# Two of the four quarters of f of both bilinear factors as 2x2 block products of seven terms, from batch 2 on

## The chip, the cores and the metric

The kernel runs on one core of one Trainium2 chip. The metric is device time in microseconds (us); three runs of the kernel before gave a median of 519.63 us (519.27 to 521.14).

## What is computed

Inputs are float32: `q`, `k`, `v` of 8 batches x 8 heads x 576 tokens x 64, `phi` with 32 memories per head, and four weight matrices (held in a 64-bit format, converted on the chip).

```python
a = exp(phi - max over tokens);  a = a / (sum over tokens + 1e-9)
k_m = einsum('bhsm,bhsd->bhmd', a, k);  v_m = einsum('bhsm,bhsd->bhmd', a, v)
attn = softmax(q @ k_m.T / 8)                 # 576 x 32 for each head
x = attn @ v_m                                # 4608 tokens x 512
out = ((x @ w1) * (x @ w2)) @ w3 @ w_out      # 512 -> 1024 -> 512
```

## The kernel before

`w3 @ w_out` is multiplied once, at the start, and so is, for each batch, `M = v_m @ [w1, w2]`: 256 rows (8 heads x 32 memories, two partition tiles t) by 2 x 1024 columns. The columns f come in four quarters of 256 (two tiles of 128), and w is 0 for w1 and 1 for w2. With the probabilities P (256 rows by 576 tokens, two halves n of 288) each batch then needs a = M1.T P and b = M2.T P, their product g = a * b (1024 x 576), and the output W.T g. Float32 precision is had from three matmuls in float32r for each product: every operand is held as a high part (a cast by ScalarE) and a low part (the rest, by VectorE), and high x high, high x low and low x high are added in PSUM. One such matmul is 128x128 by 288 columns.

For each batch, PE does two things that matter here. In the **A stage**, 16 units `A` (`ab_unit`, L589) for 8 tiles of f and 2 halves of tokens: 12 matmuls into a pair of PSUM banks (w = 0 and w = 1). ScalarE copies bank 0 to SBUF (token `a`, `a_sb`, L609), VectorE multiplies it with bank 1 into `g` (token `g`, L612). In the **O stage**, 14 units `O` (`out_unit`, L654) of 12 matmuls: the output product is already done by Winograd's form of Strassen's scheme, with sums of g on GpSimd (`f` at L618, `S1` to `S4` at L630 to L634), high and low parts of g (`h` ScalarE L646, `l` VectorE L652), results added and stored (`C11` to `C22`, L701).

Between these stand the steps of the next batch's attention and weights: `top` (L186, maximum of phi), `exp`, `bm`/`bs` (L209, L213), `be` (L217), `mem` (L227, L236), `norm`, `memc` (L248), `block`, `blockc` (L263, L264); `sc0`/`sc1` scores (L277), `scc` (L289), then the softmax `mx sb ex sm mu tr` (L294 to L317), `ah`/`al` its high and low parts (L322, L326); `M0` to `M3` (L350), `Mh` (L361) and `Ml` (L369).

The order on every engine is written by hand: FIRST (batch 0), SECOND (batch 1) and BATCH (batches 2 to 7) are lists of such tokens, and each engine takes its own in the list's order. A number b + 1 or b + 2 (prefix `+`) says for which batch a step is done, `-` the present one. All loads and stores are on SP's queue, in the list's order too.

PSUM has eight banks: two pairs `o` and `x`, one buffer each, and four banks `ab` given out from a list in the order in which they come free (`free_banks`, L123; `done`, L119). A unit `A` takes two: one comes free with its `a`, one with its `g`.

Of the kernel before, what the change touches and what calls it, by code (L numbers as in the profile page):

```python
# [33 lines left out]
f3 s2 E3 bm g g bs w1 y1 h2 A a A D0 t2 g l2 Et1 E0 S2 z2 be mem A exp norm D1 E1 memc a a l0 g g block O blockc w0
y0 h1 l1 h4 h3 t3 l4 t1 z1 z3 M0 sc0 scc0 mx0 sb0 O O l3 O O Mh0 h6 S3 S1 l6 h5 Ml0 l5 O S4 h7 p4 p1 h11 ex0 l7 O O
h9 h8 C11 sm0 mu0 tr0 l8 sc1 q2 M1 l9 O u2 ah0 h10 l10 O h12 p5 Mh1 h13 scc1 l11 al0 l12 l13 O O O O C21 C22 Ml1 mx1
sb1 ex1 C12 sm1
# [3 lines left out]
be a g A a A mem norm memc g phi2 l0 a A block g a blockc A M0 kv2 a +top g sc0 M1 g scc0 Mh1 f1 h1 A f3 mx0 sb0 A a
f2 a Ml1 ex0 g g sm0 Mh0 A +bm Ml0 a A O a A g h3 h2 +bs l1 g M2 a mu0 l3 +exp +be g sc1 Mh2 S3 l2 M3 scc1 mx1 S2 h4
+mem Ml2 O S1 l4 h5 +norm O p1 O O sb1 ex1 l5 h6 O Mh3 +memc h8 sm1 h7 S4 u2 l6 h9 tr0 O l7 l8 C11 h10 l9 l10 O p5 O
h11 h12 mu1 +block ah0 O O l11 al0 tr1 h13 l13 l12 O q2 C22 C12 +blockc Ml3 ah1 O O al1 C21
# [14 lines left out]
def memory_attention__then__bilinear_ffn_kernel(  # L59
# [84 lines left out]
    def load_phi(b):  # L144
        t = att.tile([P, NT, S], F32, name="ph", tag="ph")
        nc.sync.dma_start(out=t, in_=phiT[b].rearrange("t p s -> p t s"))
        a = att.tile([P, 9 * P], F32, name="a", tag="a")
        nc.sync.dma_start(out=a, in_=phi_tok[b])
        loaded["ph", b] = t, a

    def load_kv(b):
        t = []
        for i in range(0, 4, 2):
# [3 lines left out]
            t += [x[:, j] for j in range(2)]  # L157
# [689 lines left out]
```

## Time and profile before

| | us |
|---|---|
| median of 3 runs | 519.63 |
| the profiled execution | 520.16 |
| its span, first to last instruction | 518.4 |
| PE busy in it | 507.8 |
| VectorE (DVE) busy | 383.8 |
| ScalarE (ACT) busy | 279.9 |
| GpSimd (POOL) busy | 149.6 |

Batches begin, by the chain of waits, at 130.56 (batch 1), 192.75 (2), 248.10 (3), 303.44 (4), 358.77 (5), 414.12 (6) and 466.91 (7). A busy time is a sum over the instructions of an engine; matmuls overlap, so the length of a stretch of the chain divided by its matmuls says what one costs, and the mean duration of one does not. On VectorE, too, an instruction begins before the end of the one before it when nothing holds it; what one costs in a full queue is the distance between starts.

### The profile page before, as it was taken

How to read it: one execution, taken by the hardware profiler on the slowest of the kernel's cores; microseconds unless marked ns; L12 is line 12 of the kernel's file. 1: busy time of each engine (PE TensorE's matmuls, PEld its weight loads, DVE VectorE, ACT ScalarE, POOL GpSimd, SP SyncE). 2: the span in 40 equal slices, each digit the busy share in tenths (PEclk: the TensorE clock that was granted, in tenths of full speed). 3: DMA queues.
4: the chain of work that ended last, by engine and by line, in shares of the span. 5: the costliest groups of instructions: out<-in, count | busy, mean ns of one | idle time of the engine just before them, and what ended most of it. 6: DMA issues, size and time to landing. Idle time of an engine off the chain costs nothing.

```text
span 518.4 us, 10996 instructions
## 1 busy us (share of the span) xinstructions
PE 507.8 (98%) x4488; PEld 443.3 (86%) x4488; DVE 383.8 (74%) x647; ACT 279.9 (54%) x494; POOL 149.6 (29%) x158
## 2 busy tenths in 40 slices
PE   7998999999999999999999999999999999999997
PEld 6344459899788998989988998999898989899996
DVE  4878989889869985769566976688577936893363
ACT  6876989864436643645364625373355425543352
POOL 0005005763020801163023602080207111721280
PEclk9999999999999999999999999999999999999999
DMA  8999943603853048004810263006600400010002
GB/s 280 413 406 362 387 172 108 227 1 127 283 189 136 1 161 296 1 2 138 290 31 1 92 229 138 2 4 207 248 1 1 162 24 1 0 60 34 2 3 91
DMA packets 29795, 68.87 MB, mean 133 GB/s; under 512 B 1840, under 2 KB 10032, under 8 KB 29744
## 3 DMA queue, kind: packets, MB, share of 16 engines
q1 hardware_dynamic: 29744, 68.16, 36.9%
q8 instruction: 35, 0.57, 0.5%
q14 instruction: 16, 0.13, 0.1%
HBM read 58.72 MB, written 9.44 MB: 131 GB/s over the span
## 4 chain that ended last, share of the span: by engine, by line
PE 93%; DMA 3%; DVE 1%; issue 1%; ACT 1%; SPq 0%; ACTq 0%; DVEq 0%
PE ab L600 40%; PE o L668 19%; PE x L668 10%; PE ab L668 5%; PE ab L350 3%; PE x L502 3%; PE x L227 3%; DMA raw<-in_w_out 2%; PE o L502 2%; PE ab L502 2%; PE o L350 1%; PE x L350 1%; PE ab L277 1%; DMA raw<-in_w3T 1%; PE x L277 1%
## 5 line engine op out<-in xcount | busy, mean ns | idle before, releaser
L600 PE MATMUL ab<-ah,mh 128*128 128x288 f32 x512 | 152.5, 298 | 0.0
L600 PE MATMUL ab<-al,mh 128*128 128x288 f32 x512 | 151.1, 295 | 1.0 <-DVE al L326 1.0
L600 PE MATMUL ab<-ah,ml 128*128 128x288 f32 x512 | 151.0, 295 | 0.0
L612 DVE TENSOR_TENSOR g<-ab,a_sb 128x288 f32<-128x288 f32 x128 | 57.6, 455 | 71.2 <-PE ab L600 66.3
L609 ACT COPY a_sb<-ab 128x288 f32<-128x288 f32 x128 | 51.2, 401 | 99.5 <-PE ab L600 96.3
L600 PEld LDWEIGHTS ab<-ah,mh 128*128 128x128 f32 x512 | 96.2, 188 | 8.2 <-issue 5.7
L600 PEld LDWEIGHTS ab<-al,mh 128*128 128x128 f32 x512 | 96.3, 188 | 1.5 <-DVE al L326 1.2
L600 PEld LDWEIGHTS ab<-ah,ml 128*128 128x128 f32 x512 | 96.2, 188 | 0.0
L652 DVE TENSOR_TENSOR sl<-g,sh 128x576 fp32r<-128x576 f32 x98 | 83.2, 873 | 6.8 <-ACT sh L646 6.6
L618 POOL TENSOR_TENSOR g<-g,g 128x288 f32<-128x288 f32 x32 | 29.6, 932 | 200.1 <-DVE g L612 200.1
L646 ACT CAST sh<-g 128x576 fp32r<-128x576 f32 x98 | 65.4, 678 | 33.9 <-PE o L668 14.0
L668 PE MATMUL o<-sh,Wh 128*128 128x288 f32 x248 | 74.0, 298 | 0.0
L668 PE MATMUL o<-sh,Wl 128*128 128x288 f32 x248 | 73.2, 295 | 0.0
L668 PE MATMUL o<-sl,Wh 128*128 128x288 f32 x248 | 73.1, 295 | 0.0
L630 POOL TENSOR_TENSOR q<-g,g 128x288 f32<-128x288 f32 x28 | 22.2, 819 | 101.4 <-PE x L277 91.5
L668 PEld LDWEIGHTS o<-sh,Wh 128*128 128x128 f32 x248 | 46.6, 188 | 4.9 <-issue 4.4
L668 PEld LDWEIGHTS o<-sh,Wl 128*128 128x128 f32 x248 | 46.7, 188 | 0.0
L668 PEld LDWEIGHTS o<-sl,Wh 128*128 128x128 f32 x248 | 46.6, 188 | 0.0
L668 PE MATMUL x<-sl,Wh 128*128 128x288 f32 x136 | 40.1, 295 | 0.0
L668 PE MATMUL x<-sh,Wl 128*128 128x288 f32 x136 | 40.1, 295 | 0.0
L668 PE MATMUL x<-sh,Wh 128*128 128x288 f32 x136 | 40.0, 294 | 0.0
L634 POOL TENSOR_TENSOR g<-g,q 128x288 f32<-128x288 f32 x28 | 34.9, 1275 | 0.0
(132 smaller groups left out, 887.2 us busy)
## 6 DMA issues: line engine op xcount, KB each, us to landing
kv<-in_kv SPq DMA_DIRECT2D x16, 1024.0 KB, 9.4
q<-in_qT SPq DMA_DIRECT2D x8, 1152.0 KB, 5.5
outT<-c SPq DMA_DIRECT2D x31, 288.0 KB, 2.4
raw<-in_w3T SPq DMA_DIRECT2D x6, 1024.0 KB, 11.4
ph<-in_phiT SPq DMA_DIRECT2D x8, 576.0 KB, 5.0
a<-in_phi_tok SPq DMA_DIRECT2D x8, 576.0 KB, 5.9
raw<-in_w SPq DMA_DIRECT2D x4, 1024.0 KB, 15.5
kv<-in_w SPq DMA_DIRECT2D x3, 1024.0 KB, 14.3
```

The lines of the kernel that those rows point to most:

```text
L227: nc.tensor.matmul(ps[t][h * M : (h + 1) * M, : 2 * D], lhsT=v["a"][:, (NT * i + t) * P + h * M : (NT * i + t) * P + (h + 1) * M], rhs=kvt ...
L350: nc.tensor.matmul(ps[t][g * M : (g + 1) * M], lhsT=vm[b % 2][d, g], rhs=w12_sb[q][d, :, g], start=True, stop=True,)
L502: nc.tensor.matmul(pw[r][i][:, cols], lhsT=x[:, i * P : (i + 1) * P], rhs=wos[k // half][:, k % half, cols], start=k == 0 and cols.start == 0,
L600: nc.tensor.matmul(banks[w][:, :HALF], lhsT=x[:, t, w, fc : fc + P], rhs=y[:, n, t * HALF : (t + 1) * HALF], start=i == 0, stop=i == len(t ...
L609: nc.scalar.copy(out=a_sb, in_=banks[0][:, :HALF])
L612: nc.vector.tensor_tensor(out=G[n, f // half][:, f % half], in0=banks[1][:, :HALF], in1=a_sb, op=ALU.mult)
L618: nc.gpsimd.tensor_tensor(out=low, in0=top, in1=low, op=ALU.subtract)
L630: gp(out=s2, in0=a22, in1=s3, op=ALU.subtract)
L634: gp(out=a12, in0=a12, in1=s2, op=ALU.subtract)
L646: nc.scalar.copy(out=hi, in_=src)
L652: nc.vector.tensor_tensor(out=lo, in0=src, in1=hi.bitcast(F32), op=ALU.subtract)
L668: nc.tensor.matmul(ps[j][:, :HALF], lhsT=piece(x, s, 2 * part + k)[:, jc], rhs=y[:, k], start=i in first and part == 0 and k == 0 and t == ...
```

## The change

From batch 2 on, only f quarters 0 and 1 are done by units `A` (8 of them). In quarters 2 and 3 the contraction halves t, the f tiles u and the token halves n make 2x2 blocks, and Winograd's form of Strassen's scheme takes seven block products for eight. A product `P1` to `P7` is 6 matmuls (2 w, 3 parts). They gather in three pairs of banks: alpha takes P1, then P6, P7 and P4 on top, gamma takes P5, then P3, beta takes P2. Between the steps ScalarE copies what has gathered (`k10`: product 1, w 0), VectorE adds (`e`), and `v` multiplies into g, from two kept copies (`v1`, `v2`, `v4`) or from a bank (`v3`, after a ScalarE copy `e30`).

The scheme needs sums of both operands: of the probabilities (`T1` to `T4` in place, VectorE; `Th` and `Tl` their high and low parts) and of M (`Mr`, `Ms`, `Mt`, `Mu`: a copy, three VectorE sums of 256 columns, high and low parts of 768 columns). One sum of M is made with M itself: part of the stored weights is replaced by a difference, once for each quarter, in batch 1 (token `Q`).

Room is made by sharing: the scores' tile `s_sb` lies in the buffer of `ph`, `kvm` in that of `kv4`, M's sums of quarter 2 in that of `kv0` (so k and v are loaded in two tokens, `kvx` and `kvy`), sums under way in the buffer of `q`, together with S2. `phi` and its token form load by separate tokens. The casts of T take buffers of `sh` and `sl`, four each, from those of `h` and `l`. SECOND and BATCH are new orders; FIRST differs by the new load tokens alone.

```diff
 BATCH = """
-A phi2 a A g A a g a A g a +top A a A g g +bm a h0 A +bs g a g M0 sc0 l0 M1 +exp scc0 A a g mx0 A a Mh1 Mh0 g Ml1 A
...
+sc0 M1 f0 -Tl1 g Mh0 g Mh1 scc0 Ml0 P1 k10 Ml1 mx0 kvx2 k11 P5 P6 k51 k50 P2 sb0 k20 P3 e10 k21 +be P5 e11 ex0 e20
...
-            v["kvm"] = att.tile([P, NT, 2 * D], F32, name="kvm")
+            x = att.tile([P, NG * 2 * D], F32, name="kvm", tag="kv4")
...
+                s_sb = att.tile([P, NT, S], F32, name="s_sb", tag="ph")
...
+        def prob_sums(i):
+            (x11, x21), (x12, x22) = [[v["at"][:, n, t * HALF : (t + 1) * HALF] for t in range(NT)] for n in range(2)]
+            out, in0, in1 = {1: (x11, x12, x11), 3: (x12, x22, x12), 2: (x22, x22, x11), 4: (x21, x21, x22)}[i]
+            nc.vector.tensor_tensor(out=out, in0=in0, in1=in1, op=ALU.subtract)
+        def sums_high(n):
+            hi = big.tile([P, 2, HALF], F32R, name="sh", tag="sh", bufs=4)
+            nc.scalar.copy(out=hi, in_=v["at"][:, n].rearrange("p (t s) -> p t s", t=NT))
+        def sums_low(n):
+            lo = big.tile([P, 2, HALF], F32R, name="sl", tag="sl", bufs=4)
+            nc.vector.tensor_tensor(out=lo, in0=src, in1=hi.bitcast(F32), op=ALU.subtract)
...
+        def block_sums(tmp, q):
+            if ("tmp", q) not in ms:
+                nc.scalar.copy(out=tmp[:, 0], in_=s3)
+                return
+            for j, x, y, op in ((1, x22, 0, ALU.subtract), (0, x11, 1, ALU.add), (2, x12, 1, ALU.subtract)):
+                nc.vector.tensor_tensor(out=tmp[:, j], in0=x, in1=tmp[:, y], op=op)
...
+    def block_product(b, i, q, G):
+        bank = {2: "beta", 5: "gamma", 3: "gamma"}.get(i, "alpha")
+        if i in (1, 2, 5):
+            G[bank, q] = pair_x() if i == 2 else pair_o() if i == 5 and q == NQ - 1 else pair_ab()
+        for w in range(2):
+            for k, (x, y) in enumerate(((0, 0), (0, 1), (1, 0))):
+                nc.tensor.matmul(G[bank, q][w][:, :HALF], lhsT=xs[x][:, w], rhs=ys[y],
...
+    def block_keep(i, w, q, G):
+        nc.scalar.copy(out=G["kept", i, q][:, w], in_=G["gamma" if i == 5 else "alpha", q][w][:, :HALF])
+    def block_result(i, w, q, G):
+        bank, kept = {1: ("beta", 1), 2: ("gamma", 2), 4: ("alpha", 5)}[i]
+        nc.vector.tensor_tensor(out=c, in0=G[bank, q][w][:, :HALF], in1=c, op=ALU.add)
+    def block_g(i, q, G):
+        nc.vector.tensor_tensor(out=G[n, 1][:, 2 * (q - NQ + 2) + u], in0=x, in1=y, op=ALU.mult)
...
-            ends = ((2, 4, 6, 8), (4, 6, 8))[min(b, 1)]
+            ends = ((2, 4, 6, 8), (4, 6, 8))[min(b, 1)] if b < FIRST_BLOCKS else (4,)
...
+                elif what == "Q":
+                    x = w12_sb[quarter(what)][D:]
+                    nc.vector.tensor_tensor(out=x[:, :, :, P:], in0=x[:, :, :, :P], in1=x[:, :, :, P:], op=ALU.subtract)
```

Three places of the order follow, each in batch 3. First ScalarE in the A stage, from the two copies `a` (`a_sb`) of units 7 and 8 on, before:

```order
L609 COPY a_sb<-ab 128x288 x2
L361 CAST mh_3138<-x 128x1024
L361 CAST mh_3140<-o 128x1024
L609 COPY a_sb<-ab 128x288
L217 ACTIVATE a<-a 128x1152
L609 COPY a_sb<-ab 128x288
L302 ACTIVATE s_sb<-s_sb 128x576
```

and now, to the first copy `e30`:

```order
L664 COPY a_sb<-ab 128x288 x2
L392 CAST mh_3174<-o 128x1024
L392 CAST mh_3177<-x 128x1024
L707 COPY c<-ab 128x288 x6
L226 ACTIVATE a<-a 128x1152
L313 ACTIVATE s_sb<-s_sb 128x576
L707 COPY c<-o 128x288 x2
L707 COPY c<-ab 128x288 x2
L712 COPY a_sb<-ab 128x288
```

M0 and M1 have changed places in `o` and `x`, and ten copies of products (`c`, L707) stand where single `a_sb` copies stood. Second, VectorE in the same stretch, before:

```order
L369 TENSOR_TENSOR ml_3143<-x,mh_3138 128x1024
L298 TENSOR_TENSOR s_sb<-s_sb,st_3120 128x576
L612 TENSOR_TENSOR g_2931<-ab,a_sb 128x288
L612 TENSOR_TENSOR g_2933<-ab,a_sb 128x288 x2
L369 TENSOR_TENSOR ml_3221<-o,mh_3140 128x1024
```

and now (L717 is `e`, L727 is `v`):

```order
L667 TENSOR_TENSOR g_2975<-ab,a_sb 128x288 x2
L300 STREAM_TRANSPOSE s_sb<-ab 128x288 x2
L400 TENSOR_TENSOR ml_3182<-o,mh_3174 128x1024
L400 TENSOR_TENSOR ml_3194<-x,mh_3177 128x1024
L305 TENSOR_REDUCE st_3196<-s_sb 128x18
L309 TENSOR_TENSOR s_sb<-s_sb,st_3196 128x576
L717 TENSOR_TENSOR c<-x,c 128x288 x2
L717 TENSOR_TENSOR c<-ab,c 128x288
L727 TENSOR_TENSOR g_2974<-c 128x288
L717 TENSOR_TENSOR c<-ab,c 128x288 x2
```

Both `Ml` now come before the first `e`, and sums and products follow each other without an `A` between. Third, VectorE at the end of the batch and into the next one's first products, before:

```order
L326 TENSOR_TENSOR al<-at,ah 128x576
L317 STREAM_TRANSPOSE at<-s_sb 128x576
L701 TENSOR_TENSOR c<-x,c 128x576
L326 TENSOR_TENSOR al<-at,ah 128x576
L369 TENSOR_TENSOR ml_3643<-ab,mh_3386 128x512 x2
L263 TENSOR_SCALAR km_75<-ab 64x128
```

and now:

```order
L424 TENSOR_TENSOR msl<-q,msh 128x768
L323 TENSOR_TENSOR s_sb<-s_sb,ss_3663 128x576
L400 TENSOR_TENSOR ml_3681<-ab,mh_3660 128x512 x2
L273 TENSOR_SCALAR km_75<-ab 64x128
L274 COPY vm_77<-ab 64x128
L273 TENSOR_SCALAR km_75<-ab 64x128
L274 COPY vm_77<-ab 64x128
L328 STREAM_TRANSPOSE at<-s_sb 128x576
L815 TENSOR_TENSOR c<-x,c 128x576
L337 TENSOR_TENSOR al<-at,ah 128x576
L667 TENSOR_TENSOR g_3722<-ab,a_sb 128x288 x3
```

The softmax's last steps (L323, L328, L337) and the low part of M's sums now stand at the very end, `Ml3` and `blockc` ahead of them.

## Rows read from the trace of the kernel before

**Rows 1.** The page: busy time by engine, share of the span, instructions.

```profile
PE 507.8 (98%) x4488; PEld 443.3 (86%) x4488; DVE 383.8 (74%) x647; ACT 279.9 (54%) x494; POOL 149.6 (29%) x158
```

**Rows 2.** Windows by batch (1, 3, 6, 7): length, busy time of each engine, clock.

```profile
137.70:192.75 55.05, 53.67 (x588) 48.98 (x587) 46.89 (x81) 29.00 (x56) 14.44 (x16) 1.00 0.43 151
...
248.10:303.44 55.34, 55.34 (x542) 51.71 (x542) 41.04 (x72) 26.55 (x51) 16.00 (x16) 1.00 0.31 108
...
414.12:466.91 52.79, 52.79 (x459) 49.29 (x458) 37.82 (x65) 23.67 (x44) 16.03 (x16) 1.00 0.07 23
466.91:518.40 51.49, 47.60 (x360) 47.36 (x359) 21.99 (x35) 18.38 (x36) 16.10 (x16) 0.99 0.09 30
```

**Rows 3.** Windows, the two halves of batch 3, the same columns.

```profile
248.10:275.50 27.40, 27.40 (x238) 25.74 (x238) 17.70 (x35) 13.40 (x27) 3.63 (x4) 1.00 0.41 141
275.50:303.44 27.94, 27.94 (x306) 25.97 (x306) 23.33 (x37) 13.15 (x24) 12.37 (x12) 1.00 0.22 75
```

**Rows 4.** The chain in order of time, batch 3: start, length, engine, line, count.

```profile
248.10 9.52 PE ab L600 x72
...
277.86 1.88 PE x L227 x64
...
280.61 1.72 PE ab L350 x32
```

**Rows 5.** Groups by form, whole span: busy, mean ns of one, idle before, releaser.

```profile
L612 DVE TENSOR_TENSOR g<-ab,a_sb 128x288 f32<-128x288 f32 x128 | 57.6, 455 | 71.2 <-PE ab L600 66.3 <-ACT a_sb L609 4.4
L609 ACT COPY a_sb<-ab 128x288 f32<-128x288 f32 x128 | 51.2, 401 | 99.5 <-PE ab L600 96.3 <-DVE g L612 2.8
...
L361 ACT CAST mh<-x 128x1024 fp32r<-128x1024 f32 x7 | 7.1, 1019 | 2.8 <-PE x L350 2.8
```

**Rows 6.** Timeline of VectorE, batch 3: start, length (of x2: of both).

```profile
259.62 0.82 DVE L612 TENSOR_TENSOR g<-ab,a_sb 128x288 f32<-128x288 f32 x2
260.36 0.75 DVE L652 TENSOR_TENSOR sl<-g,sh 128x576 fp32r<-128x576 f32 x1
...
265.76 1.23 DVE L369 TENSOR_TENSOR ml<-x,mh 128x1024 fp32r<-128x1024 f32 x1
266.90 0.75 DVE L298 TENSOR_TENSOR s_sb<-s_sb,st 128x576 f32<-128x576 f32 x1
...
298.01 1.42 DVE L652 TENSOR_TENSOR sl<-g,sh 128x576 fp32r<-128x576 f32 x2
299.35 0.75 DVE L326 TENSOR_TENSOR al<-at,ah 128x576 fp32r<-128x576 f32 x1
```

**Rows 7.** Timeline of batch 4's O stage: GpSimd's sums and VectorE beside them.

```profile
336.16 3.09 POOL L630 TENSOR_TENSOR q<-g,g 128x288 f32<-128x288 f32 x4 [15.02 <-PE x L277]
...
338.51 1.29 DVE L369 TENSOR_TENSOR ml<-ab,mh 128x512 fp32r<-128x512 f32 x2 [0.94 <-ACT mh L361]
...
343.34 5.19 POOL L634 TENSOR_TENSOR g<-g,q 128x288 f32<-128x288 f32 x4
...
343.92 3.94 DVE L652 TENSOR_TENSOR sl<-g,sh 128x576 fp32r<-128x576 f32 x3
```

**Rows 8.** Timeline of batch 4's begin: first matmul, first copy, first product.

```profile
303.27 0.29 PE L600 MATMUL ab<-ah,mh 128*128 128x288 f32 x1
...
304.26 0.40 ACT L609 COPY a_sb<-ab 128x288 f32<-128x288 f32 x1 [0.15 <-PE ab L600]
...
305.13 0.46 DVE L612 TENSOR_TENSOR g<-ab,a_sb 128x288 f32<-128x288 f32 x1 [0.64 <-PE ab L600]
```

**Rows 9.** The chain at the begin of batch 1.

```profile
139.33 0.76 DVE al L326
```

**Rows 10.** The page's DMA issues: count, KB each, median us to landing.

```profile
kv<-in_kv SPq DMA_DIRECT2D x16, 1024.0 KB, 9.4
q<-in_qT SPq DMA_DIRECT2D x8, 1152.0 KB, 5.5
...
ph<-in_phiT SPq DMA_DIRECT2D x8, 576.0 KB, 5.0
```

More of the change, by code (lines that the diff above doesn't have):

```diff
@@ L34 @@
[L34 to L37, printed above, removed]
+-mu1 -tr1 C1 -ah0 -al0 W12 W13 W14 W15 W16 M0 Mh0 M1 C3 -ah1 Mh1 C2 W17 C4 Ml0 Ml1 Dt0 C4 A a -al1 g phi1 tok1 A A
+C2 a C3 a Et0 Dt3 g C5 g s3 f0 C1 C5 A A t0 Kh2 Kl2 a a g Et3 C2 M2 Mh2 Dt2 Dt1 g Ml2 A a A C1 C4 g f1 F3 F2 F0 a
@@ L38 @@
+top g C3 r2 q1 A a A C1 a C5 g g C3 C4 C5 kv1 F1 f2 z0 A A D2 a a Kl0 D3 w2 y2 M3 Mh3 g g E2 Et2 Ml3 w3 A A h0 a a
+Kl3 y3 f3 s2 E3 bm g g bs w1 y1 h2 A a A D0 t2 g l2 Et1 E0 S2 z2 be mem A exp norm D1 E1 memc a a l0 g g block O
+blockc w0 y0 h1 l1 h4 h3 t3 l4 t1 z1 z3 M0 sc0 scc0 mx0 sb0 O O l3 O O Mh0 h6 S3 S1 l6 h5 Ml0 l5 O S4 h7 p4 p1 h11
+ex0 l7 O O h9 h8 C11 sm0 mu0 tr0 l8 sc1 q2 M1 l9 O u2 ah0 h10 l10 O h12 p5 Mh1 h13 scc1 l11 al0 l12 l13 O O O O C21
+C22 Ml1 mx1 sb1 ex1 C12 sm1
 """
 SECOND = """
-A a A -mu1 g -tr1 a -M3 g -M2 phi1 A -ah1 top -al1 a kv1 -Mh3 A -Ml3 a -Mh2 h0 g g -Ml2 A a g bm f0 exp bs A a g A
@@ L41 @@
[L41 to L44, printed above, removed]
+-mu1 A A tok1 a -tr1 g -M2 a -M3 A -ah1 -Mh3 -Mh2 a A Q -al1 g g a g -Ml3 phi1 A A top a g bm a bs g kv1 exp A A
@@ L45 @@
+phi2 -Ml2 Q f0 a be mem g A norm memc block a h0 g A a tok2 blockc +top M1 a g sc0 +exp g scc0 M0 mx0 A A Mh1 l0 kv2
+a f2 g a f1 sb0 ex0 f3 Ml1 A sm0 a Mh0 A g a A g Ml0 +bm g A +norm O mu0 +bs a h1 h2 l1 h3 a l3 l2 tr0 +be sc1 M2
++mem g g M3 Mr Ms O Mh2 S2 S3 scc1 Mt Ml2 mx1 h4 +memc O Mu S1 l4 h6 p1 h5 l5 l6 S4 Mr O O ah0 h8 O h7 Ms u2 C11 l7
+O +block h13 h9 l8 sb1 Mt O ex1 h10 Mh3 l9 Mu l10 al0 O p5 O l13 h11 l11 O sm1 O h12 q2 C22 l12 mu1 tr1 Ml3 O
++blockc ah1 O C21 al1 C12
 """
 BATCH = """
-A phi2 a A g A a g a A g a +top A a A g g +bm a h0 A +bs g a g M0 sc0 l0 M1 +exp scc0 A a g mx0 A a Mh1 Mh0 g Ml1 A
@@ L48 @@
-a A f0 +be sb0 g a kv2 A ex0 a g A g Ml0 h2 f2 h1 A a g O a A l1 g sm0 h3 l3 A a g mu0 +mem sc1 f3 +norm a l2 M3 g
-f1 M2 S2 scc1 Mh3 Mh2 tr0 S3 Ml2 O h9 S1 h4 O mx1 +memc O p1 l4 O h5 l5 S4 O h6 h7 sb1 l6 h8 O l7 O ex1 l8 u2 sm1
-h10 l9 l10 q2 p5 mu1 O h12 O h11 ah0 O l11 O C11 C22 h13 +block l13 l12 O al0 tr1 ah1 O C12 al1 Ml3 +blockc C21
+A A a a g A g a g -T1 h0 phi2 tok2 -T3 A -T2 a g A l0 a -T4 g +top A A -Th1 +bm -Th0 h1 a g +exp A -Tl0 M0 +bs a a
+sc0 M1 f0 -Tl1 g Mh0 g Mh1 scc0 Ml0 P1 k10 Ml1 mx0 kvx2 k11 P5 P6 k51 k50 P2 sb0 k20 P3 e10 k21 +be P5 e11 ex0 e20
@@ L51 @@
+v1 k50 e21 P7 P1 f2 k51 e40 v2 e41 sm0 k11 v4 k10 P4 l1 P3 P6 P2 e30 v3 k20 e20 k21 f1 f3 e21 P7 mu0 h2 e40 v2 e41 O
+e11 e10 P4 v4 v1 e30 v3 M2 sc1 M3 h3 l2 l3 kvy2 Mh2 Mr +mem Ms S2 +norm h4 +memc O Ml2 S3 p1 l4 h5 Mt tr0 O S1 O h6
+S4 scc1 l5 Mu ah0 h8 O l6 Mr h7 O mx1 u2 O l7 C11 h10 O l8 h9 Ms h11 l9 O p5 O l10 l11 h12 sb1 O +block al0 Mt h13
+l12 C22 l13 ex1 Mh3 sm1 O Mu mu1 Ml3 +blockc q2 O tr1 ah1 C12 O C21 al1
 """
@@ L156, in load_kv @@
             nc.sync.dma_start(out=x, in_=src)
[L157 removed]
+            t |= {i + j: x[:, j] for j in range(2)}
+        if 4 not in parts:
+            return
         x = att.tile([P, NG * 2 * D], F32, name="kv4", tag="kv4")
@@ L616, in first_sum @@
+    def block_g(i, q, G):
+        n, u = (i - 1) % 2, (i - 1) // 2
+        if i == 3:
+            x, y = G["alpha", q][1][:, :HALF], G["a_sb", q]
+        else:
+            x, y = (G["kept", {1: 1, 2: 2, 4: 5}[i], q][:, w] for w in range(2))
+        nc.vector.tensor_tensor(out=G[n, 1][:, 2 * (q - NQ + 2) + u], in0=x, in1=y, op=ALU.mult)
+        if i == 3:
+            G["alpha", q].done(1)
     def first_sum(k, G):
```

108 lines of the change are left out of this document (90 added, 18 removed).

## The prediction

> **What bounds the kernel now.** I read the page first, then windows by batch, then the chain, then VectorE's timeline. PE is busy 507.8 of 518.4 us [rows 1], and the granted clock is 1.00 in every batch's window but the last, 0.99 [rows 2]. By windows, PE has no idle time at all in batches 2 to 6: the row of batch 3 stands for batches 2 to 5, which all take 55.33 to 55.35 us with PE busy throughout [rows 2]. In the chain nearly everything is PE, matmuls back to back: 72 in 9.52 us, 0.132 us each [rows 4]. So time is what PE has to issue, and what the change has to be held against is the next engine: VectorE is busy 41.04 of a batch's 55.34 us [rows 2], 17.70 of 27.40 in the A stage and 23.33 of 27.94 in the O stage [rows 3]. ScalarE (26.55) and GpSimd (16.00) have far more room.
>
> **What is removed.** In each of batches 2 to 7 two quarters go from 48 to 42 matmuls. That is 12 x 0.132 = 1.59 us a batch, six times: 9.5 us, all of it on the path, if nothing new makes PE wait. Batch 3 would take 55.34 - 1.59 = 53.75 us.
>
> **What VectorE gets.** In a full queue, two products g and the next instruction start 0.74 us apart (259.62 to 260.36), so a 288-column instruction costs 0.37; two of 576 columns take from 298.01 to 299.35, 0.67 each; 1024 columns cost 1.14 (265.76 to 266.90) [rows 6]. From 0.37 and 0.67, 1.04 ns a column and 0.07 for the instruction. For each batch:
> - products: 6 `e` and 4 `v` for 4 `g` in each quarter, 12 more x 0.37 = 4.4 us
> - T1 to T4, 4 x 0.37 = 1.5; Tl, 2 x 0.67 = 1.3
> - `Ms`, 2 x 3 of 256 columns: each waits for the one before, so up to the full 0.455 of a 288-column row [rows 5] less 32 columns, 0.42: 2.5
> - `Mu`, 2 x 768 columns, 0.67 + 192 x 1.04 ns = 0.87: 1.7.
>
> Together 11.4 us: 41.0 + 11.4 = 52.4 us of VectorE in 53.75. That is 98%, and it decides the case. The sums over the batch say that it can fit; whether it does is a matter of order, so I follow VectorE's queue against PE's by stage.
>
> A stage, from the first unit to M2: PE has 8 units (12.7), `bm` 0.3, M0 and M1 0.86 each by half of the row of 1.72 [rows 4], sc0 0.5, 84 matmuls of the products (11.1) and the first O (1.6): 28 us. VectorE's list there, by columns: 8 g 3.0, T and Tl 2.8, top 1.3, bs 1.75 (1024 columns and two short ones), l0 and l1 1.3, scc0 0.8, two Ml 2.3, mx0, sb0, sm0, mu0 3.3, 12 e and 8 v 7.4: 23.9 us. O stage, M2 to the end: PE M2, sc1, M3 2.2, mem 1.9 [rows 4] and 0.4 for its tail, 13 O 20.6, block 0.3: 25.4 us. VectorE's list adds up to 28.4 us: 12 l, two Ms, two Mu, two Ml, three C, al0, al1, tr0, tr1, scc1, mx1, sb1, sm1, mu1, norm, blockc, by the same rows, with 3.2 us for GpSimd's company (next paragraph) and 0.45 of waiting for Mr. So VectorE makes up 4 us in the A stage and falls back 3 in the O stage: I have it end its list about 3.4 us after PE's last O of the batch (57.6 against 54.2 from the first unit).
>
> Is 3.4 us of delay paid for? The begin of a batch shows the rhythm [rows 8]: the copy `a` starts 0.99 us after its unit, the product 1.86 after. The first two units take banks that Ml3, C11 and blockc set free, all ahead of the last five VectorE instructions of the new list. The third takes the two banks that ScalarE's copies free. Only the fourth, 3 x 1.59 = 4.8 us after the batch's begin, needs a product g, so VectorE may be up to 4.8 - 0.46 = 4.3 us late. 3.4 stays 0.9 below. `al1`, last of all, is wanted by the fifth unit only.
>
> **GpSimd beside VectorE.** With GpSimd's sums running, three `sl` take 3.94 us, 1.31 each where 0.67 is usual, and a group of four sums stretches from 3.09 to 5.19 [rows 7]. In batch 3 six such instructions meet the sums; in the new list l4, l5, the first Mu, l6, l7 and part of l3 do, 3.2 us in all. An instruction with a PSUM input keeps its pace: two Ml of 512 columns take 1.29 us beside the first sums [rows 7], 0.6 each by columns. So do e, Ms and v3, I take it. [...]
>
> **New waits on PE.** Three places have little room. P2's bank pair `x` is that of M1, set free by the second Ml. That waits for the second Mh, a ScalarE cast of 1.02 us [rows 5] after M1, and ends 2.6 us after M1; P1, P5 and P6 cover 2.4: 0.26 us. P1 of quarter 3 takes gamma's banks, free with `e21`, which I find 0.26 us ahead of need; the first O takes pair `o` after `e21` of quarter 3, 0.25 ahead. In the O stage l6, l7 and l9, behind the contended instructions, come 0.05 to 0.3 late, 0.45 us together. That makes 0.7 us by exact walk; unseen semaphore times are not in it and neither is the cover of waits that overlap, and I take 0.6. Batches 2 to 5 then gain 1.59 - 0.6 = 1.0 us each, 4.0.
>
> Batches 6 and 7 have less beside the products: without top, bs, norm and blockc VectorE has 4.4 us less in batch 6, and 22 of 51 us are busy in batch 7 before [rows 2]. I take gains of 1.3 and 1.5 us. In batch 7 S2 can start as soon as v2 and v4 are done, since no scores hold the buffer of q, so S1 isn't late.
>
> **Batch 1 and the loads.** Batch 1 gets two Q of 1024 columns (2.3 us) and M's sums (4.2) on a VectorE busy 46.89 of 55.05 us [rows 2], so 53.4; but al1, which held PE until 140.13 [rows 9], now stands ahead of top, worth some 1 us. The scores of batch 2 need the exponentials of batch 3 done first, since ph and s_sb share a buffer: about 1 us late by my reckoning. I take 0, from -1.2 to +1.5. Loads: ph waits for tr1 of the batch before and lands 5 us after its issue, 7.7 after the begin; top stands at 8.6. q lands at 4.4, wanted at 14.0. kvy can go once P3 of quarter 2 is done (19.6) and takes up to 9.4 [rows 10]; mem comes at 30.6. SP has nothing else behind these that is sooner due. All cost nothing with one to two microseconds of cover, phi the least.
>
> ScalarE gets 6 more copies, casts of T and of M's sums, about 6 us on 26.55: hidden, apart from the places named.
>
> **The sum.** 4.0 + 1.3 + 1.5 = 6.8 us off the profiled 520.16, so 513.4; that execution lies 0.5 above the median of 519.63, and I give **513.0 us**.
>
> **The rivals.**
> - *VectorE becomes the bound.* [...] If v, T, Tl and Mu mostly meet GpSimd, 10 x 0.37 + 2 x 0.67 + 2 x 0.87 = 6.8 us a batch would be doubled at worst; half of it, 3.4 us, makes VectorE 6.8 us late at the batch's end, 2.5 over the limit of 4.3. Then batches 2 to 5 lose 2.5 - 1.0 = 1.5 each, 6 - 2.8 = +3.2: 523 us. It turns slower than before from 2.6 us a batch over my list (0.9 of margin, 1.0 of gain, 0.7 for the gain of batches 6 and 7). For: 98% load, margins under half a microsecond. Against: in the order `f0` to `f3` are free to run beside Ml (PSUM input), and my list for the batch before, 37.1 + 4.0 for contention, gives the 41.04 of the row.
> - *The products wait for their own banks.* alpha is used four times, and between P1 and P6, P6 and P7, P7 and P4 two copies or sums must pass. Cover is one product, 0.8 us, or more; two copies take 0.2 + 0.7. If the copies stand behind Mh or `be` (1.0 to 1.2 us), 0.5 us is lost at some three of the six places: the gain of 1.59 is gone, and the time is 518 to 519.6, no change. [...]
> - *PE stays full.* All waits vanish, batch 1 keeps its 1 us: 519.6 - 9.5 - 1 = 509 to 510.
>
> **Chances.** Forecast 0.57, PE full 0.13, products wait 0.18, VectorE bound 0.12. The range runs from the inside of the second case to that of the third, 509.5 to 519.5, and so leaves out little but the fourth and the end of the second. A measurement can tell about 0.5%, 2.6 us: under 517.0 counts as faster, which holds the first two cases; the third and a tenth of the fourth are within 0.5%: faster 0.70, same 0.19, slower 0.11.
>
> **What would show it.** Right: batches 2 to 5 at 54.0 to 54.6 us by the chain, PE groups of 288 columns 72 fewer, VectorE busy near 52 us in each batch, its last step 3 to 4 us after the last O, ph's landing not waited for. Wrong: PE waiting for g at the fourth unit of a batch (VectorE bound), or for `c` copies ahead of P6, P7, P4 (products wait), or VectorE's v and T at twice 0.37 us; for batch 1, PE waiting for s_sb.

## The result, and the profile after

The kernel after takes 511.99 us (median of 4 runs, 511.43 to 514.38) against 520.04 for the kernel before beside it: a ratio of 0.985, interval 0.982 to 0.989. It is faster, by 8.0 us: less than 2%, but the interval is clear of 1. Its profiled execution took 511.91 with a span of 510.1; that of before had 518.4. The page answers to [rows 1]:

```profile
PE 500.6 (98%) x4416; PEld 434.6 (85%) x4416; DVE 446.4 (88%) x805; ACT 311.5 (61%) x566; POOL 147.2 (29%) x158
```

TensorE has 72 matmuls less, VectorE 158 instructions and 62.6 us more. The windows of batches 1, 3, 6 and 7 and the two halves of batch 3 answer to [rows 2, 3], with the same columns:

```profile
131.10:191.91 60.81, 60.81 (x658) 54.42 (x658) 55.93 (x99) 34.62 (x65) 14.78 (x16) 1.00 0.44 156
245.96:300.01 54.05, 54.05 (x530) 50.09 (x530) 50.92 (x97) 31.77 (x63) 15.40 (x16) 1.00 0.33 111
408.11:460.02 51.91, 51.52 (x447) 47.79 (x446) 46.28 (x89) 28.76 (x56) 16.02 (x16) 1.00 0.12 42
460.02:510.10 50.08, 46.05 (x348) 45.81 (x347) 32.07 (x56) 21.78 (x45) 16.76 (x16) 0.99 0.10 36
245.96:274.34 28.38, 28.38 (x250) 26.36 (x256) 26.00 (x54) 17.01 (x37) 3.15 (x4) 1.00 0.53 179
274.34:300.01 25.67, 25.67 (x288) 23.73 (x289) 24.92 (x44) 14.77 (x27) 12.25 (x12) 1.00 0.11 35
```

VectorE is at 94% of a steady batch and TensorE still waits for almost nothing. By the begins of the batches in the chains, batch 1 went from 62.19 to 60.81 us, batches 2 to 5 from 55.34 to 54.05 each (1.29 less), batch 6 from 52.79 to 51.91, batch 7 to its last matmul from 47.61 to 46.06. Batch 1 began 0.54 later, because the first unit of batch 0 did (74.06 against 73.53, both batches 0 then take 56.87). What stands ahead of it is the same but for the split load, and in the traces of the runs below whose batch 0 is that of after, batch 1 began anywhere between 130.4 and 131.3, so this is spread. Sum: 1.38 + 4 x 1.29 + 0.88 + 1.55 - 0.54 = 8.4 us to the last matmul; the spans differ by 8.3.

The full 1.59 us are not there: 0.30 us a batch are missing. The chain of batch 3 (start, length, what) shows where:

```profile
261.25 2.58 PE ab L695 x18
263.83 0.96 PE x L695 x6
264.79 0.80 PE ab L695 x6
...
274.34 1.02 PE ab L381 x16
275.36 0.48 PE x L285 x16
275.84 0.86 PE ab L381 x16
```

```profile
262.47 1.21 DVE L400 TENSOR_TENSOR ml<-x,mh 128x1024 fp32r<-128x1024 f32 x1
```

A product of six matmuls takes 0.80; P2, the one into `x`, takes 0.96, for it waits for the second Ml (0.17), which ends at 263.68; P2's first matmul starts at 263.73. And M2, sc1, M3 take 2.36 together where sc1 and both M took 0.48 + 1.72 before [rows 4 has the 1.72]: 0.16 more. These two come to 0.33, a little over the 0.30, for the kernel before had a small wait of its own in this batch (one pair of O units took 3.24, the others 3.17).

VectorE at the end of batch 3 and the sums of GpSimd that it meets:

```profile
276.91 1.21 DVE L412 TENSOR_TENSOR q<-ab,q 128x256 f32<-128x256 f32 x3 [0.49 <-ACT q L409]
...
282.77 1.54 DVE L424 TENSOR_TENSOR ms<-q,ms 128x768 fp32r<-128x768 f32 x1
284.24 1.37 DVE L766 TENSOR_TENSOR sl<-g,sh 128x576 fp32r<-128x576 f32 x1
...
301.74 0.76 DVE L337 TENSOR_TENSOR al<-at,ah 128x576 fp32r<-128x576 f32 x1
302.58 0.46 DVE L667 TENSOR_TENSOR g<-ab,a_sb 128x288 f32<-128x288 f32 x1
```
```profile
279.31 4.19 POOL L746 TENSOR_TENSOR g<-q,g 128x288 f32<-128x288 f32 x4
283.46 4.93 POOL L748 TENSOR_TENSOR g<-g,q 128x288 f32<-128x288 f32 x4
```

Batch 4 begins at 300.01; its first product g starts 2.57 us later. In the kernel before it was 1.69, by the same begin of 303.44 (the 1.86 of [rows 8] runs from the first matmul at 303.27, which starts before the last of the batch before has ended). In batch 6, which has no `mem`, the chain leaves TensorE ahead of its third O:

```profile
438.79 0.43 DVE q L412
...
439.24 0.75 DVE q L412 x2
440.00 0.61 DVE ml L400
...
440.74 3.41 PE ab L782 x24
```

TensorE stands still for 0.39 us there (busy 51.52 of 51.91): the O unit takes M2's banks, which `Ms` and Ml2 must have read.

### The profile page after: what moved, and what is told of

The parts are those of the page before. It is cut to its first block, busy times and chain, and to the rows that moved or that the text cites. A ratio compares the mean times of both kernels' runs of the same rounds, so it can differ in the third digit from the quotient of the medians.

```text
span 510.1 us, 11167 instructions
## 1 busy us (share of the span) xinstructions
PE 500.6 (98%) x4416; PEld 434.6 (85%) x4416; DVE 446.4 (88%) x805; ACT 311.5 (61%) x566; POOL 147.2 (29%) x158
## 4 chain that ended last, share of the span: by engine, by line
PE 89%; DMA 7%; ACT 1%; DVE 1%; SPq 1%; issue 0%; ACTq 0%
PE ab L655 25%; PE o L782 19%; PE x L782 11%; PE ab L695 9%; PE ab L782 5%; DMA kv<-in_kv 4%; PE ab L381 3%; PE x L236 3%; DMA raw<-in_w_out 2%; PE o L557 2%; PE x L557 2%; PE x L695 2%; PE o L695 2%; PE o L381 1%; PE x L381 1%; PE ab L285 1%
## 5 line engine op out<-in xcount | busy, mean ns | idle before, releaser
L655 PE MATMUL ab<-ah,mh 128*128 128x288 f32 x320 | 95.8, 300 | 0.0
L655 PE MATMUL ab<-al,mh 128*128 128x288 f32 x320 | 94.4, 295 | 0.0
L655 PE MATMUL ab<-ah,ml 128*128 128x288 f32 x320 | 94.4, 295 | 0.0
L733 POOL TENSOR_TENSOR g<-g,g 128x288 f32<-128x288 f32 x32 | 26.2, 838 | 201.0 <-DVE g L667 196.5
L655 PEld LDWEIGHTS ab<-ah,mh 128*128 128x128 f32 x320 | 60.2, 188 | 4.2 <-DVE g L667 1.7
L655 PEld LDWEIGHTS ab<-al,mh 128*128 128x128 f32 x320 | 60.2, 188 | 0.2 <-issue 0.2
L655 PEld LDWEIGHTS ab<-ah,ml 128*128 128x128 f32 x320 | 60.2, 188 | 0.0
L664 ACT COPY a_sb<-ab 128x288 f32<-128x288 f32 x80 | 31.4, 399 | 33.9 <-PE ab L655 33.0
L667 DVE TENSOR_TENSOR g<-ab,a_sb 128x288 f32<-128x288 f32 x80 | 35.6, 453 | 18.4 <-PE ab L655 13.7
```

The lines of the kernel that those rows point to most:

```text
L655: nc.tensor.matmul(banks[w][:, :HALF], lhsT=x[:, t, w, fc : fc + P], rhs=y[:, n, t * HALF : (t + 1) * HALF], start=i == 0, stop=i == len(t ...
L664: nc.scalar.copy(out=a_sb, in_=banks[0][:, :HALF])
L667: nc.vector.tensor_tensor(out=G[n, f // half][:, f % half], in0=banks[1][:, :HALF], in1=a_sb, op=ALU.mult)
L733: nc.gpsimd.tensor_tensor(out=low, in0=top, in1=low, op=ALU.subtract)
```

## The experiments

My theory after the result: TensorE has no room, so a matmul removed is 0.13 us gained; VectorE may end its list late up to a limit at a batch's begin; batch 1's gain is the moved al1. The rivals are those of the prediction. Profiled executions are compared by the lengths of their batches: where a run changes nothing in them, batches 2 to 5 took 54.03 to 54.06 us in every trace but for one batch (54.34, under "Loads free" below).

**The matmuls put back.** In `block_product`:

```diff
+                for _ in range(2 if i in (1, 2, 5) and k == 0 else 1):
                     nc.tensor.matmul(
```

> The kernel after, with the first matmul of each accumulation in the banks of P1, P2 and P5 issued twice (start is set, so the second writes the same again): 12 matmuls more in each of batches 2 to 7, so that TensorE issues as many as in the kernel before, while VectorE's list, the order and the loads stay those of after. Theory (TensorE has no room, the gain is the 72 matmuls): +12 x 0.132 = 1.59 us a batch, batches 2 to 5 from 54.05 to 55.6, in all +9.5: about 521.5 us, a little above the kernel before in spite of the better batch 1. Rival (VectorE sets the batch, or the gain came from the order and the loads): the matmuls fit into time in which TensorE waits anyway, batches 2 to 5 stay under 54.5 and the whole under 515.

Measured: 520.19 us (before beside it 518.98), batches 2 to 5 at 55.48 to 55.49, batch 6 at 53.38. From its chain of batch 3:

```profile
262.16 3.12 PE ab L696 x22
265.28 1.06 PE x L696 x8
```

Four more matmuls cost 0.54 in the first row, but two more in P2 only 0.10, since P2's wait covers the rest. So 1.43 of 1.59 come back: the gain of batches 2 to 7 is the matmuls, and in batches 2 to 5 the order, the loads and the VectorE work added cost nothing beyond the 0.3 us named above. (Batch 6 is 0.6 longer than in the kernel before with its matmuls back, mostly by the wait ahead of its third O.)

**VectorE made later, a little and a lot.** In `probs_low`, with 3 and then 7 for k:

```diff
+            for _ in range(k if n == 1 and b > 2 else 1):
                 nc.vector.tensor_tensor(out=lo, in0=v["at"][:, n], in1=hi.bitcast(F32), op=ALU.subtract)
```

> The kernel after, with al1, the last step of VectorE's list of a batch, issued three times in place of once at the ends of batches 2 to 6: 2 x 0.69 = 1.4 us more of VectorE a batch, 50.9 + 1.4 = 52.3 of 54.05. Theory (a queue that may end 4.3 us late and ends 2.6 us late, the first g of batch 4 starting 2.57 us after the batch's begin): it then starts 3.95 us after, inside the limit; batches 3 to 6 stay within 0.15 of 54.05 and 51.91, the whole stays at 512 within a measurement's spread. Rival (VectorE has no room left, a microsecond on it is a microsecond of the batch): +1.4 at each of five boundaries, 54.05 to 55.4, the whole 519.

> The same with al1 seven times: 6 x 0.69 = 4.1 us more of VectorE at each of five boundaries, 55.0 of work where a batch took 54.05. Theory (the limit is a lateness of 4.3 us at a batch's begin): the first g starts 6.7 us after the begin, 2.4 beyond the limit, and the fourth unit A waits that long: batches 3 to 5 at 56.4, the whole at 512 + 5 x 2.4 = 524. Rival 1 (throughput is what counts, lateness is averaged out over the batch): batches at VectorE's work, 55.0 to 55.3, the whole 517. Rival 2 (every microsecond costs one): 58.1, the whole 532.

Measured with 3: 511.63 us, batches 2 to 6 at 54.05, 54.03, 54.06, 54.06 and 51.92: nothing. Batch 4 begins at 299.70 there, and VectorE's timeline has

```profile
301.43 2.35 DVE L338 TENSOR_TENSOR al<-at,ah 128x576 fp32r<-128x576 f32 x3
303.69 0.45 DVE L668 TENSOR_TENSOR g<-ab,a_sb 128x288 f32<-128x288 f32 x1
```

so the first g 3.99 us late is free. With 7: 532.85 us. Batch 3 begins at 245.71, the first g starts at 252.88, 7.2 us later (the repeats stand 0.79 apart, not 0.69), and TensorE's timeline shows the fourth unit behind it:

```profile
250.18 0.29 PE L656 MATMUL ab<-ah,ml 128*128 128x288 f32 x1
253.38 0.41 PE L656 MATMUL ab<-ah,mh 128*128 128x288 f32 x1 [2.90 <-DVE g L668]
```

7.2 less 2.9 is 4.3: the limit of the prediction, measured. The waits are 2.6 to 2.9 at each of five boundaries, 14.2 us. Most of the other 6.7 us goes with the clock. Over the 4 us behind the five waits the granted clock was 1.00, 0.60, 0.50, 0.59 and 1.00. The first row is of the work behind the wait above; the next two are the wait of the batch after it and the work behind that (clock: third number from the end):

```profile
253.38:260.00 6.62, 6.62 (x51) 6.62 (x51) 6.18 (x12) 5.18 (x11) 0.81 (x1) 1.00 0.57 206
...
307.60:310.62 3.02, 0.11 (x2) 0.01 (x1) 2.92 (x6) 0.00 (x0) 0.00 (x0) 0.96 0.95 324
310.62:314.60 3.98, 3.98 (x19) 3.98 (x20) 2.67 (x7) 1.38 (x3) 0.00 (x0) 0.60 0.99 369
```

Behind the second wait the granted clock is 0.60 on average over 4 us, and 48 matmuls take 8.03 us where 6.62 were taken behind the first wait. That is 1.41 more; three boundaries with such a clock make 4.2 of the 6.7, an estimate. So the theory's mechanism holds and its price for crossing the limit was too low; rival 2's 532 came out by another way than its own.

**al1 alone.** In SECOND of the kernel before:

```diff
-A a A -mu1 g -tr1 a -M3 g -M2 phi1 A -ah1 top -al1 a kv1 -Mh3 A -Ml3 a -Mh2 h0 g g -Ml2 A a g bm f0 exp bs A a g A
+A a A -mu1 g -tr1 a -M3 g -M2 phi1 A -ah1 -al1 top a kv1 -Mh3 A -Ml3 a -Mh2 h0 g g -Ml2 A a g bm f0 exp bs A a g A
```

> The kernel before with one step moved in batch 1's order: al1 ahead of top on VectorE, as the kernel after has it, and nothing else of the change. Theory (the 1.38 us that batch 1 gained are TensorE's wait for al1 behind top, which waited for phi's load): batch 1 from 62.19 to 60.8 to 61.2, all other batches as before (55.34), the whole 1.0 to 1.4 under the kernel before. Rival (batch 1 gained by the other moves of its order or by the split load): batch 1 stays at 62.2 within 0.2.

Measured: batch 1 from 130.47 to 191.35, 60.88 us, 1.31 less than in the kernel before; the others at 55.34. The wait of [rows 9] is gone, and the chain at that place is matmuls alone:

```profile
135.52 4.96 PE ab L600 x36
```

That is batch 1's gain, and it has nothing to do with Strassen's scheme. (The whole, 518.77 beside 518.98, is one run of each and can't show 1.3 us.)

**More of GpSimd beside the products.** In `first_sum`:

```diff
+        for _ in range(3):
             nc.gpsimd.tensor_tensor(out=low, in0=top, in1=low, op=ALU.subtract)
```

> The kernel after with each of GpSimd's first sums f0 to f3 of a batch issued three times (they subtract in place, so three times is once): 8 x 0.77 = 6.2 us more of GpSimd in each A stage. In batch 3 of after f1 to f3 end at 262.7, beside VectorE's two Ml; now they reach 267 to 268, beside sb0, e and the first v. Theory (two inputs in SBUF meet GpSimd's at about twice their time, one input in PSUM does not): sb0 1.3 to 1.4 in place of 0.76, v1 and v2 0.7 in place of 0.45, e unchanged at 0.45; 1.3 to 2 us of VectorE, which the A stage has spare, and batches 2 to 5 grow by at most 0.5. Rival 1 of the prediction (VectorE has nothing spare where products wait for it): each microsecond of contention is one of the batch, 55.5 to 56, the whole 520 or more.

Measured: 521.02 us, above the rival's 520, but batches 2 to 5 at 54.48, 0.43 more; most of the rest is in batch 0 (4.7) and batch 1 (62.94, of which more below). In batch 3, sb0 took 0.88 and v1 0.74 in place of 0.45, 0.41 us of delay in all; v2, which started 0.09 us ahead of a sum, kept 0.44, and that sum took 1.02 where one takes 0.81. TensorE pays for the delay at two places:

```profile
273.07 0.74 DVE L727 TENSOR_TENSOR g<-c 128x288 f32<-128x288 f32 x1
273.74 0.81 DVE L717 TENSOR_TENSOR c<-ab,c 128x288 f32<-128x288 f32 x2
...
274.83 0.45 DVE L717 TENSOR_TENSOR c<-ab,c 128x288 f32<-128x288 f32 x1
```
```profile
274.24 0.40 PE L695 MATMUL ab<-ah,mh 128*128 128x288 f32 x1
...
275.33 0.40 PE L695 MATMUL ab<-sh,mh 128*128 128x288 f32 x1
```

These are the second halves of P1 of quarter 3 and of P4 of quarter 2. Each starts 0.05 to 0.06 us after the `e` whose bank it takes: e21, the first of the two at 273.74, ends at 274.18, and e41 at 275.28. In after the same `e` are

```profile
266.50 0.81 DVE L717 TENSOR_TENSOR c<-ab,c 128x288 f32<-128x288 f32 x2
...
267.60 0.45 DVE L717 TENSOR_TENSOR c<-ab,c 128x288 f32<-128x288 f32 x1
```

e21 ends at 266.95 and e41 at 268.05, and the two matmuls start at 267.42 and 268.21: 0.47 and 0.16 us of margin, no more. The theory's bound held, its reason ("the A stage has it spare") did not: there VectorE is not late on average, but at these two places a few tenths of a microsecond count.

**S1 and S4 left out.** In `sums`:

```diff
+            if 1 < b and which in ("S1", "S4"):
+                a, a12, s2 = (x[:, :8] for x in (a, a12, s2))
```

> The kernel after with S1 and S4 of GpSimd cut to 8 of 288 columns from batch 2 on, so that those sums are left out of the output: 8 of 12 sums of the O stage are gone. Theory (contention is paid by VectorE's spare time): the three steps that meet them, Mu 1.54, sl 1.37 and sl 1.41, fall to 0.85, 0.7 and 0.7, VectorE's list ends 2.0 us earlier, the first g of a batch starts 0.6 to 1 us after the begin in place of 2.57, and batches 2 to 5 stay at 54.05 within 0.1; the whole 512. Rival (contention delays what TensorE waits for): batches 2 to 5 fall by 0.3 or more, the whole to 510 or less.

Measured: 512.67 us (a span of 509.8), batches 2 to 5 at 54.05 to 54.06. Mu took 0.96 and no sl more than 0.84, so contention had cost 1.7 us of VectorE a batch (49.23 busy against 50.92). Yet the list ended only 0.4 us earlier, the first g 2.13 after the begin, for a wait took its place:

```profile
285.87 0.76 DVE L768 TENSOR_TENSOR sl<-g,sh 128x576 fp32r<-128x576 f32 x1 [1.13 <-ACT sh L762]
```

The low parts wait for ScalarE's high parts, whose four buffers come free with the O units (this high part itself waits 0.64 us for an O unit). TensorE paces VectorE there, so contention in that place is paid out of a wait.

**M2 and M3 together.** In BATCH, and for batch 6 alone:

```diff
-e11 e10 P4 v4 v1 e30 v3 M2 sc1 M3 h3 l2 l3 kvy2 Mh2 Mr +mem Ms S2 +norm h4 +memc O Ml2 S3 p1 l4 h5 Mt tr0 O S1 O h6
+e11 e10 P4 v4 v1 e30 v3 M2 M3 sc1 h3 l2 l3 kvy2 Mh2 Mr +mem Ms S2 +norm h4 +memc O Ml2 S3 p1 l4 h5 Mt tr0 O S1 O h6
...
+            if b == B - 2:
+                text = text.replace("Ms S2 +norm h4 +memc O Ml2", "S2 +norm h4 +memc O Ml2 Ms")
```

> The kernel after with two moves: M2 and M3 next to each other on TensorE and sc1 behind them (after has sc1 between, and the two then take 1.02 + 0.86 where the kernel before has 1.72 for both), and in batch 6 alone Ms on VectorE behind Ml2 in place of ahead of it. Theory (TensorE has no room; the 0.30 us that batches 2 to 5 lack of the full 1.59 are these 0.16 and P2's 0.17): batches 2 to 5 from 54.05 to 53.89, batch 6 from 51.91 by 0.16 and the 0.39 that TensorE stands idle at 440.35 to 51.4, the whole 1.2 us less, 510.8. Rival (sc1 later, or Ms later, makes VectorE's list late): batches at 54.05 or more, the whole 512 or more.

Measured: 512.22 us (511.79 to 515.76), ratio to before 0.987, interval 0.985 to 0.989: no better than after. Batches 2 to 5 at 54.05, batch 6 at 52.49, 0.58 more. The theory fell twice:

```profile
273.68 1.88 PE ab L381 x32
275.56 0.49 PE x L285 x16
```

Both M take 1.88 even side by side; they took 1.72 before, where the scores and the 64-row end of `mem` had come ahead of them. So the 0.16 seems to be a price of going from 128-row matmuls to these 64-row ones (sixteen M take 1.02 behind the former, 0.86 behind scores); in these traces it is due once for each run of them, wherever sc1 stands. The kernel before has one such run there (the end of `mem`, sc1, M2, M3), after has two, since M2 to M3 stand ahead of `mem`. Batch 6 has no `mem`, so one run in either kernel, and there sc1, M2 and M3 take 2.36 us in both, from their first start to that of the O unit behind. And in batch 6 `Ms` reads the same M2 banks, so O waits for it on either side of Ml2; it now also started later.

**P5 ahead of P2.** On top of that:

```diff
-... k11 P5 P6 k51 k50 P2 sb0 k20 P3 e10 k21 +be P5 e11 ex0 e20
+... k11 P5 P6 k51 k50 P5 P2 sb0 k20 P3 e10 k21 +be e11 ex0 e20
```

> As the run before, and in each of batches 2 to 7 P5 of quarter 3 moved ahead of P2 of quarter 2 on TensorE, so that P2 comes 0.8 us later to the bank that the second Ml sets free. Theory: P2's 0.17 us go, batches 2 to 5 at 53.7 to 53.75, the whole 0.8 to 1.0 less than the run before, 509.9. Rival (P2's products wait, and VectorE stands still for 0.5 us ahead of e10): the products behind it come late for their copies and the gain is gone or turned, batches at 53.9 to 54.3.

Measured: 515.57 us (514.61 to 518.1), ratio 0.993, interval 0.991 to 0.994; batches 2 to 5 at 54.54. The rival came true, and beyond its numbers. P2's wait is gone, and in its place TensorE waits at the two places of the run with more of GpSimd. The chain of batch 3 goes through VectorE at the first and stops at the second, 271.41, where e41 ends at 271.36:

```profile
269.44 0.44 DVE g L727
269.89 0.38 DVE c L717
270.27 0.04 issue
270.31 1.05 PE ab L695 x6
271.37 0.04 issue
271.41 0.66 PE ab L695 x3
```

VectorE had stood still 0.39 us ahead of e10, and that is what the batch grew by, and a little more. The profiled run had something else as well: batch 1 took 62.95, as with three f. VectorE and GpSimd in its O stage:

```profile
172.90 4.53 DVE L424 TENSOR_TENSOR ms<-q,ms 128x768 fp32r<-128x768 f32 x1
```
```profile
170.42 3.14 POOL L746 TENSOR_TENSOR g<-q,g 128x288 f32<-128x288 f32 x4
173.50 3.12 POOL L748 TENSOR_TENSOR g<-g,q 128x288 f32<-128x288 f32 x4
```

Mu begins beside S1 and ends 0.8 us after S4, 4.53 us where it takes 1.4 to 1.5 in the other traces (4.53 again in the run with three f), and GpSimd isn't slowed at all. TensorE loses 2.13 us in batch 1. Where in a sum Mu starts doesn't decide it: 0.16 and 0.19 us after the start of S1's last sum in these two traces, 0.14 to 0.19 in eight others that have the same sums.

**The contention by itself.** At the end of the last batch's list 32 sums on GpSimd, and on VectorE 24 steps of 576 columns, in fours: two SBUF inputs, a reduction of one, one PSUM and one SBUF input, two SBUF inputs, the reduction, two SBUF inputs:

```diff
+        for _ in range(8):
+            for k in range(half):
+                nc.gpsimd.tensor_tensor(out=low[:, k], in0=top[:, k], in1=low[:, k], op=ALU.subtract)
```

> The kernel after with work put behind the last batch that the output doesn't need: 32 of GpSimd's sums of 288 columns, back to back, and beside them on VectorE six groups of four steps of 576 columns: two SBUF inputs, a reduction with one SBUF input, one PSUM and one SBUF input, two SBUF inputs, the reduction, two SBUF inputs. It measures the contention by itself; the batches stay as they are, and the whole grows by the tail, 25 to 45 us. Theory 1 (the two engines take turns, instruction by instruction): a step with two SBUF inputs takes 1.3 to 1.5 in place of 0.67, GpSimd's sums beside it 1.2 to 1.5 in place of 0.78; the reductions and the PSUM steps stay at 0.67 to 0.75, GpSimd's at 0.78 beside them. Theory 2 (a step that comes while GpSimd is at work stands until GpSimd's queue runs dry, as the 4.53 us of Mu in batch 1 of the run with P5 ahead of P2 look like): the first two-input step takes up to 25 us and all others are undisturbed.

Measured: 531.29 us, 19 more than after and not 25 to 45, for GpSimd began its sums at 495.5, beside the last O units. By VectorE's timeline:

```profile
503.24 4.77 DVE L942 TENSOR_TENSOR g<-g,g 128x576 f32<-128x576 f32 x4
507.94 3.10 DVE L938 TENSOR_REDUCE mx<-g 128x2 f32<-128x576 f32 x4
510.96 2.74 DVE L940 TENSOR_TENSOR g<-x,g 128x576 f32<-128x576 f32 x4
513.62 4.72 DVE L942 TENSOR_TENSOR g<-g,g 128x576 f32<-128x576 f32 x4
```

By the starts, a step with two SBUF inputs takes 1.17 us on average, 0.88 for the first of a group and 1.27 for those behind it; a reduction 0.75, one with a PSUM input 0.67. GpSimd's 32 took 33.0, that is 1.27 each beside the steps with two SBUF inputs and 0.75 beside the others. So the two take turns in this run, at 1.27 us each, and a step with one SBUF input (0.75) or a PSUM input (0.67) is left alone. The 4.53 us are not what this run shows.

**Whether the shut-out makes the upper times.** After again; S1 and S4 cut in batch 1 alone; and a small step on GpSimd that makes S4 of batch 1 wait for Mu:

```diff
+        if b == 1 and which == "S4":
+            x = ready["M", 2]["sums", 2][1][:, 0, 0, :8].bitcast(F32)
+            gp(out=att.tile([P, 8], F32, name="gate"), in0=x, in1=x, op=ALU.subtract)
```

> The kernel after, unchanged, beside the next run on the same chip, for the spread of its times: four runs gave 511.43 to 512.07 and one of them 514.38. Theory (in batch 1 Mu or the sl behind it is now and then shut out while GpSimd does S1 and S4, 2.13 us of TensorE in the two traces that show it): most runs at 511.4 to 512.2, one in three to five 2 to 2.5 us above. Rival (the spread is the clock or the loads): times spread evenly, or no such group.

> The kernel after with S1 and S4 cut to 8 of 288 columns in batch 1 alone, left out of the output there. Theory (S1 and S4 of batch 1 are what shuts VectorE out): no run of the upper group, all at 511.3 to 512.2, batch 1 at 60.8. Rival: as many runs at 514 and above as in the run before.

> The kernel after with one small step on GpSimd ahead of S4 in batch 1 (8 columns, reading what Mu of quarter 2 writes), so that S4 can't begin before Mu is done: GpSimd then has a gap at the end of S1 in which VectorE's Mu gets through. In two traces Mu took 4.53 us, beginning beside S1 and ending 0.8 us after the end of S4, in the others 1.46, ending 0.8 us after the end of S1. Theory (VectorE's step waits for the run of GpSimd's sums that is on to end, and S4 behind S1 without a gap sometimes keeps it out): Mu 1.46 in the profiled run, batch 1 at 60.8, and no time of the upper group: 511.0 to 512.7, median 511.6. Rival (the upper times have another cause): one or two of six runs at 514 or above, as of after (514.38 of four runs, 514.14 of five).

Measured: after 510.98, 512.16, 512.67, 513.16, 514.14 (ratio 0.986); without S1 and S4 511.15 to 512.24 in four runs (0.984); with S4 behind Mu 511.26, 511.52, 512.12, 512.83 (0.986, interval 0.984 to 0.988). Batch 1 was 60.80 to 60.81 in all three traces. Three of 15 runs with the batch 1 of after (four, these five, six with M2 and M3 together) were above 514, none of the eight in which S1 and S4 are cut or S4 waits for Mu. The spans, first to last instruction, separate them better: 512.4, 512.6 and 513.5 us for the three, 509.2 to 510.9 for the other twelve, 509.2 to 510.5 for the eight. The 513.16 has a span of 510.0 and an undisturbed batch 1 (Mu 1.48) in its trace, so it isn't of the upper group. The clock doesn't sort them: 0.996 to 0.999 on average in the three, 0.996 in one of the eight too, with a span of 510.2. That fits the shut-out but isn't proof: eight runs would miss one in five about one time in six, and none of the three was traced. What decides between 1.46 and 4.53 stays open. None of these versions is measurably faster than after.

## Why the prediction was right

- **Forecast 513.0, measured 511.99.** The case came true that I held likeliest: TensorE still the bound, VectorE late but inside its limit. That the sum is so near is in part luck: batches 2 to 5 together were 1.2 us better than forecast and batch 1 1.4, batch 6 was 0.4 worse and the start 0.5.
- **Matmuls, 1.59 a batch.** Right: putting them back cost 1.43, and the other 0.16 is hidden in P2's wait.
- **VectorE's list, 52.4 us.** 50.92 measured. Pieces of the new work fitted: Ms 1.21 for three against 1.26, Mu 0.9 undisturbed, `e` and `v` 0.37 apart. The term that was too big is GpSimd's company: 3.2 forecast, 1.7 by the run without S1 and S4. I counted five steps and a part that meet the sums at twice their time; three did. Beside S2 and S3 stood `Ms` and Ml2, which read PSUM, beside S1 a transpose and scc1, and three more sl beside sums kept 0.72 to 0.82.
- **3.4 us late of 4.3 allowed.** Measured 2.5 (al1 ends at 302.50, the last O at 300.01), and the limit is 4.3 by the seven al1. The step that turned out weaker is the link from contention to lateness: I let it add up to the end of the batch, while 1.1 of the 1.7 us vanish in a wait for ScalarE's high parts.
- **Waits on TensorE, 0.6 a batch.** 0.30 measured. P2 0.17 for 0.26; no wait at P1 (e21 ends 0.47 ahead, I had found 0.26), at the first O or for l6, l7, l9; but 0.16 for M2, sc1 and M3, now ahead of `mem`, which I had summed as if they cost what they did in the old order. So batches 2 to 5 gained 1.29, not 1.0.
- **Batch 6, 1.3.** 0.88: with `mem` out of the way M2 is followed by O sooner, and the chain Mh2, Mr, Ms, Ml2 holds the banks that the third O takes. I had counted VectorE's hours there, not that chain. **Batch 7, 1.5:** 1.55.
- **Batch 1, 0.** 1.38, the largest miss. I had both terms, about 1 us for al1 and about 1 us against it for scores that wait for an exponential. The first was there in full (1.31 by the run with al1 alone), the second not at all: the chain of batch 1 after is matmuls alone.
- **Loads free.** Right in batch 3: ph was issued at 248.64, landed in 4.8 and was wanted at 254.37, 0.9 us of cover. In batch 5 it took 5.6, and 0.1 was left. In the trace with the sums at the end it took 6.6 in batch 5, top waited 0.86 us, and the batch took 54.34:

```profile
356.10 6.64 DMA ph<-in_phiT
```

- **Rival "VectorE becomes the bound".** Its limit was right and not reached; 1.4 us more a batch were free, 4.8 more cost 4.2 a batch, 2.9 of them the wait and most of the rest, by the estimate above, the clock (0.50 to 0.60 behind three of the five waits).
- **Rival "products wait for their own banks".** It didn't happen, by 0.47 and 0.16 us. Two runs that delay VectorE by 0.4 in the A stage show it at two of the places that the prediction names, P1 of quarter 3 and between P7 and P4, at 0.43 and 0.49 a batch. In after, the products of the two quarters, taken in turn, hide the emptying of these banks, just so.
- **Rival "PE stays full".** Half of it came true: batch 1 kept its 1 us and more, and half of the 0.6 us of waits a batch vanished. The measured time lies between this rival's 509 to 510 and the forecast.

## What to carry to other kernels

Where one engine is full, count what it stops issuing, and then hold the next engine's queue against it by stage and not by its sum: 94% busy was harmless at the batch's end, with 1.7 us to spare, and 0.4 us of delay was paid for at two places in the middle that had 0.47 and 0.16. Read a gain batch by batch as well: 1.4 of the 8.4 us had nothing to do with the idea of the change. Before putting a wait down to contention, look at what the engine would wait for without it.
